# Buffers for split expert weights, and work of the first expert moved ahead, in a sparse attention and MoE kernel on one core

## The chip, the core and the metric

The kernel runs on one core of a Trainium2 chip. Its engines work beside one another, each on its own queue, in order: TensorE (PE) multiplies matrices, VectorE (DVE), ScalarE (ACT) and GpSimd (POOL) work on elements, and the queue of SyncE (SP) issues the DMA transfers. An engine waits for another by a semaphore. The metric is the device time of one execution in microseconds (us); a kernel is judged by the median of its runs.

## What is computed

Block-sparse attention (4 batches, 8 heads, 768 positions, head dimension 64), whose output is the input of a mixture of 8 experts. Every token goes through every expert; the gate's weights are balanced over rows and columns eight times.

```python
scores = scale * np.matmul(q, k.transpose(0, 1, 3, 2))
scores = np.where(mask, scores, -1000000000.0)
scores = scores - np.max(scores, axis=-1, keepdims=True)
attn = np.exp(scores); attn = attn / (np.sum(attn, axis=-1, keepdims=True) + 1e-09)
x = np.matmul(attn, v)                       # then (3072, 512): heads side by side
P = np.exp(x @ w_gate - max)                 # (3072, 8), eight rounds of balancing
...
for e in range(E):
    h = np.maximum(x @ w1[e], 0.0)           # 512 -> 1024
    out += P[:, e:e + 1] * (h @ w2[e])       # 1024 -> 512
```

## The kernel before

**Number form.** A float32 operand is scaled by a power of two and split into two float16 halves, high = f16(s * w) and low = f16(s * w - high). A product is three matmuls (high x high, high x low, low x high). One *split* of a weight quarter is therefore one ACT instruction for the high half and one DVE instruction for the low half.

**Seven products.** Each matrix product of the expert part is done by a seven-product scheme on 2 x 2 quarters, numbered 0 to 6, in the order 0, 1, 5, 6, 3, 4, 2 (`PORDER`). Four quarters of a weight matrix and sums of them give seven operands. The sums are made on POOL, in place over the raw quarters, so some sum must wait until an earlier split has read its quarter: the sums for products 5 and 2 of w1 wait for the splits of 0 and 1, and so do those for 5 and 3 of w2.

**Attention part (0 to 414 us).** A planner issues work tick by tick (`T`), by a table `plan_at` of fixed places and by *chains* of jobs: at the end of every tick, `deal` takes from each chain what is ready and fits an estimate of how busy DVE, ACT and POOL are. Three instructions per tile of the softmax matter here: the exp (`pe`, ACT, line 730), its low part (`pl`, on the engine that the planner thinks lightest, lines 740, 742, 744) and the matmuls with V (line 787). V's raw data lies in `vraw` (line 448). The chains load w1 and w2 of the first expert and find their scales; they sum and split all seven quarters of w1 (`first_sums`, `first_high`, `first_low`, lines 258 to 282), and make the first four of eight sums of w2 (lines 980 to 993).

**Expert part (from 414 us).** An *item* i is one expert and one batch, i = 4e + b, 32 in all. Stage 1 of an item (`stage1`, line 1315) makes the hidden values: 4 column blocks x 7 products x 6 matmuls 128x384, evacuated by DVE (line 1336) and ACT, then split into halves `h` (ACT line 1345; low half DVE line 1350 or 1356, or POOL line 1356). Stage 2 (`stage2`, line 1435) makes the outputs: 7 products x 3 row blocks x 12 matmuls 128x256, which DVE adds into the accumulator (line 1480). The main loop (line 1555) runs stage 2 of item i interleaved with stage 1 of item i + 1. Names such as `p_8_0` mean item 8, column block 0.

**Who sets the order.** `Slots` (line 1109) counts a *tick* for each product and each output block. Work beside the matmuls waits in queues: *urgent* (halves of h), *lazy* (weights: magnitudes, scale, sums, splits, in the order in which they were queued), *calm* (the last batch's x steps, then the gate's balancing). A step runs when its tick has come and the estimate of its engine isn't over TensorE's by more than 1 us. `slots.need(key)` runs at once whatever of a key is left; `stage1` does it for the w1 operand and `stage2` for the w2 operand of a product. A scheduler then orders the instructions of each engine by these places.

**Weights of the next expert.** The raw weight has one buffer (`r`), w1 and w2 in turn. In the second item of an expert (b = 1) w1 of the next is loaded, scaled, and half of its sums made (`sum_w1`). The split operands of w1 have one buffer per product (lines 231 to 242, in the memories `arena` and `attic`). So `split_w1` (line 1216) queues the split of product p only when the last column block of the expert's last stage 1 has used it (`used[p]()`, line 1329); the other sums are queued behind the splits of 0 and 1. w2 is split alike in stage 2 of the last item (`split_w2`, line 1239). For the first expert `split_w2` queues, around its first column blocks, seven splits and the last four sums (two sums of four pieces on POOL, line 1202).

**Last batch's x.** `finish_x` (line 373) makes steps for the fourth batch: differences on POOL (line 401), high halves on ACT (387), low halves on DVE (391) with a store on SP (393), and the gate's logits on TensorE (332). They are queued with delay `LATE` = 34 ticks (line 1529); balancing follows them in the same queue.

## Time and profile before

| | |
|---|---|
| median of 3 runs | 2201.07 us (2196.04 to 2204.06) |
| profiled execution | 2201.64 us |
| its span, first to last instruction | 2199.9 us |
| granted TensorE clock, mean | 0.998 |
| busy: PE, weight loads, DVE, ACT, POOL | 98%, 72%, 78%, 58%, 65% |
| DMA, mean | 87 GB/s |

A row of a group of instructions reads: line, engine, operation, output<-inputs with shapes, count | busy time, mean ns of one | idle time of the engine just before them and what ended most of it. A row of the waits reads: engine and line <- engine and line that it waited for: us in total, times, longest. A row of the timeline has the start, the length, the instruction and count, and in brackets the idle time before it with its releaser. A row of a stretch has its bounds and length, then the busy time and count of PE, weight loads, DVE, ACT and POOL, the granted clock, the DMA share and GB/s. Weight loads run beside matmuls, and the ends of matmuls are modelled.

### The profile page before, as it was taken

To read this page: it belongs to the slowest core of one execution; us is meant where nothing else is said; L and a number is where in the kernel's file an instruction comes from. 1 tells how busy PE (TensorE), PEld (TensorE's weight loads), DVE (VectorE), ACT (ScalarE), POOL (GpSimd) and SP (SyncE) were. 2 spreads that over 40 slices of the span, in tenths; PEclk is the share of its full clock that TensorE was granted. 3 is DMA by queue.
4 is the path that set the end of the run, shared out by engine and by line. 5 is a ranking of instruction groups with operands and counts; after the bars stand their busy time and mean duration, and the time that the engine had idled before them with its cause. 6 is when DMAs were issued, how large, how long until landed. Compare 5 with 4: busy or idle time off the path is not lost.

```text
span 2199.9 us, 47055 instructions
## 1 busy us (share of the span) xinstructions
PE 2150.8 (98%) x18796; PEld 1591.8 (72%) x18796; DVE 1706.8 (78%) x2970; ACT 1282.8 (58%) x2385; POOL 1432.6 (65%) x1476
## 2 busy tenths in 40 slices
PE   6999999999999999999999999999999999999999
PEld 4777676667777777777777777777777777777777
DVE  8889889677878767876887688768876887688765
ACT  5888888666466546554655465546554655465442
POOL 4667768477568656765676567656765686567553
PEclk9999999999999999999999999999999999999999
DMA  6757796122121212121212121212121212131221
GB/s 170 180 130 171 171 198 146 42 100 84 58 89 51 90 51 90 51 90 51 89 52 89 51 89 51 89 51 89 51 89 51 90 51 89 51 90 58 80 80 51
DMA packets 195632, 192.34 MB, mean 87 GB/s; under 512 B 132412, under 2 KB 150868, under 8 KB 195412
## 3 DMA queue, kind: packets, MB, share of 16 engines
q1 hardware_dynamic: 194848, 189.30, 30.6%
q8 instruction: 147, 2.41, 0.4%
q14 instruction: 73, 0.60, 0.1%
q10 hardware_dynamic: 564, 0.03, 0.0%
HBM read 140.54 MB, written 17.30 MB: 72 GB/s over the span
## 4 chain that ended last, share of the span: by engine, by line
PE 72%; DVE 11%; POOL 7%; ACT 4%; issue 4%; DMA 1%; POOLq 0%; DVEq 0%; ACTq 0%
PE py L1456 31%; PE p L1324 30%; PE u L787 3%; PE m L689 2%; PE t L722 2%; PE m L692 2%; PE t L725 2%; POOL h L1356 2%; DVE top L698 1%; ACT h L1345 1%; POOL s L1404 1%; DMA kt<-ks 1%; POOL r L1202 1%; DVE h L1356 1%; DVE attic L1191 1%
## 5 line engine op out<-in xcount | busy, mean ns | idle before, releaser
L1456 PE MATMUL py<-w2p,h 128*128 128x256 f16 x8064 | 973.2, 273 | 6.3 <-DVE acc L1480 2.6
L1456 PEld LDWEIGHTS <-h 128*128 128x128 f16 x8064 | 788.9, 98 | 159.0 <-issue 7.4
L1356 POOL TENSOR_TENSOR h<-u,h 128x384 f16<-128x384 f32 x128 | 126.4, 988 | 534.8 <-ACT h L1345 534.8
L1324 PE MATMUL p<-attic 128*128 128x384 f16 x2304 | 421.4, 326 | 3.9 <-DVE attic L1191 2.1
L1324 PEld LDWEIGHTS <-attic 128*128 128x128 f16 x3072 | 299.2, 98 | 173.1 <-DVE attic L1191 6.6
L1324 PE MATMUL p<-arena 128*128 128x384 f16 x2304 | 417.1, 326 | 4.2 <-DVE arena L1191 1.7
L1480 DVE SCALAR_TENSOR_TENSOR acc<-py,spare,acc 128x256 f32<-128x256 f32 (+1 forms) x588 | 299.8, 514 | 90.9 <-PE py L1456 85.5
L1345 ACT ACTIVATE h<-c 128x384 f16<-128x384 f32 x256 | 132.5, 518 | 348.3 <-DVE c L1336 301.2
L1324 PEld LDWEIGHTS <-arena 128*128 128x128 f16 x2304 | 224.9, 98 | 128.4 <-issue 3.5
L1336 DVE SCALAR_TENSOR_TENSOR a<-p,a 128x384 f32<-128x384 f32 x384 | 211.4, 550 | 20.8 <-PE p L1324 9.0
L1356 DVE TENSOR_TENSOR h<-s,h 128x384 f16<-128x384 f32 x128 | 113.2, 884 | 146.6 <-ACT h L1345 146.5
L698 DVE TENSOR_REDUCE top<-m 128x1 f32<-128x768 f32 x192 | 181.8, 951 | 41.0 <-PE m L692 40.3
L730 ACT ACTIVATE pe<-t,qk 128x768 int32<-128x768 f32 x192 | 172.3, 899 | 69.8 <-PE t L725 58.7
L1209 POOL TENSOR_TENSOR c<-c,r 128x384 f32<-128x384 f32 x128 | 159.1, 1243 | 10.0
L1345 ACT ACTIVATE h<-r 128x384 f16<-128x384 f32 x256 | 129.8, 516 | 60.4 <-POOL r L1209 58.8
L1209 POOL TENSOR_TENSOR r<-s,r 128x384 f32<-128x384 f32 x128 | 157.9, 1234 | 10.0
L744 POOL TENSOR_SCALAR pl<-pe 128x768 f16<-128x768 uint16 x125 | 108.9, 874 | 72.2 <-ACT pe L730 69.7
L1404 POOL TENSOR_TENSOR s<-a,u 128x384 f32<-128x384 f32 x128 | 133.0, 1039 | 30.9 <-ACT a L1401 30.1
L1356 POOL TENSOR_TENSOR h<-r,h 128x384 f16<-128x384 f32 x128 | 146.0, 1140 | 6.0 <-ACT h L1345 6.0
L1324 PE MATMUL p<-arena,attic 128*128 128x384 f16 x768 | 145.9, 326 | 0.0
L787 PE MATMUL u<-vq,pl 128*128 128x65 f16 x1152 | 142.2, 193 | 0.3 <-ACT pl L742 0.3
L689 PE MATMUL m<-kt,qt 128*128 128x512 f16 (+1 forms) x384 | 127.7, 333 | 15.2 <-DMA kt<-ks 10.9
(196 smaller groups left out, 3704.1 us busy)
## 6 DMA issues: line engine op xcount, KB each, us to landing
arena<-xd SPq DMA_DIRECT2D x128, 384.0 KB, 3.4
attic<-xd SPq DMA_DIRECT2D x96, 384.0 KB, 3.6
r<-in_moe_w_dram SPq DMA_DIRECT2D x14, 2048.0 KB, 8.6
arena<-in_q_dram SPq DMA_DIRECT2D x16, 384.0 KB, 4.2
arena<-in_k_dram SPq DMA_DIRECT2D x16, 384.0 KB, 4.6
vraw<-in_v_dram SPq DMA_DIRECT2D x16, 384.0 KB, 5.6
xd<-xs_t SPq DMA_DIRECT2D x16, 384.0 KB, 4.3
out_dram<-acc SPq DMA_DIRECT2D x48, 128.0 KB, 1.7
```

The source lines that it names most:

```text
L689: nc.tensor.matmul(sc[:, lo:hi], lhsT=qt[:, 0, c], rhs=ka[:, lo:hi], start=True, stop=False)
L698: nc.vector.tensor_reduce(out=tops[n][:, c : c + 1], in_=sc[:, :S], axis=AX.X, op=ALU.max)
L730: nc.scalar.activation(pe, sc[:, :S], AF.Exp, bias=EXP_SHIFT, scale=qk[n // 2][3])
L787: nc.tensor.matmul(uv[:, c, :n], lhsT=l[:, c * P : (c + 1) * P], rhs=w[:, h, kc, :n], start=(kc == 0 and c == 0 and m == 0), stop=(kc == N ...
L1209: nc.gpsimd.tensor_tensor(out=out, in0=x, in1=y, op=ALU.subtract)
L1324: nc.tensor.matmul(ps, lhsT=w1p[p][:, l, kc, fs], rhs=xp[p][:, r, kc], start=(kc == 0 and m == 0), stop=(kc == KH - 1 and m == 2),)
L1336: nc.vector.scalar_tensor_tensor(out=t, in0=ps, scalar=HDOWN, in1=other, op0=ALU.mult, op1=ALU.add)
L1345: nc.scalar.activation(h[:, 0], src, AF.Relu if relu else AF.Copy)
L1356: eng.tensor_tensor(out=h[:, 1], in0=src, in1=h[:, 0], op=ALU.subtract)
L1404: nc.gpsimd.tensor_tensor(out=s1, in0=a1, in1=u3, op=ALU.add)
L1456: nc.tensor.matmul(py, lhsT=hs[i, p, kc][:, l, tsl], rhs=w2p[p][:, r, kc], start=(old is None and kc == 0 and m == 0), stop=(kc == KF // 2 ...
L1480: nc.vector.scalar_tensor_tensor(out=dst, in0=src, scalar=c, in1=dst, op0=ALU.mult, op1=ALU.add)
```

## The change

Three edits. (1) Three more buffers for split w1 operands (`spares`). The operands of products 0, 1 and 6 of the next expert go into them as soon as its sums and scale are made, in its second item, with the sums for 5 and 2 in the same queue; only the splits of 5, 3, 4 and 2 follow the last products, into the buffers that products 0, 1, 5 and 6 of the old expert let go. The buffers of its 3, 4 and 2 become the next spares. (2) V's raw memory becomes a tile that lives to the end (`vault`); when the attention is done with V it holds the split w2 operands of products 1, 0 and 5. For the first expert these are split by the planner's chains, after the remaining four sums, which become jobs as well. The planning loop runs 11 ticks longer, `ROOM`. (3) `LATE` goes from 34 to 22.

```diff
-LATE = 34
+LATE = 22
+ROOM = 12
...
+    vault = ctx.enter_context(tc.tile_pool(name="vault", bufs=1)).tile(
+        [P, H * NC * D], F32, name="vault"
+    )
...
+    w2p = {
+        p: carve(4 * KB * n, F16, 2, KF // 2, DH, home=vault)
+        for n, p in enumerate((1, 0, 5))
+    }
...
-        vraw = vsp.tile([P, H, NC, D], F32, name="vraw")
+        vraw = vault.rearrange("p (h c d) -> p h c d", h=H, c=NC)
...
+            by_w2.update({0: m[0, 0], 1: m[1, 0], 5: m[0, 0]})
+            return [
+                add for out, x, y in (
+                    (t1, m[0, 1], m[0, 0]), (m[0, 1], m[0, 1], m[1, 1]),
+                    (m[0, 0], m[1, 1], t1), (m[1, 0], m[1, 0], m[0, 0]),
+                ) for add in add_kc(two(out), two(x), two(y))
+            ]
...
+        for p in (1, 0, 5):
+            until = ((("w2", "power"), 1),) + (
+                ((("w2", "sum", 5), 2),) if p == 5 else ()
+            )
+            splits += [
+                job(("w2", "high", p), lambda p=p: first_high(w2p[p], by_w2[p], 2),
+                    (0.0, 1.14, 0.0), after=until),
...
-        for T in range(min(plan_at), max(plan_at) + 1):
+        for T in range(min(plan_at), max(plan_at) + ROOM):
...
+    w1ps = {0: w1p}
+    spares = [big.tile([P, 2, KH, FH], F16, name=f"w1p_{n}") for n in range(3)]
+    follows = {}
...
     def split_w1(e):
         a, s3 = wr["a"], wr["s3"]
+        old = w1ps[e - 1]
+        new = w1ps[e] = {p: spares.pop(0) for p in (0, 1, 6)}
...
+        one(0, a[0, 0])
+        queue_sum(a[0, 0], a[1, 0], a[0, 0], ("w1", e, 5))
+        one(1, a[0, 1])
+        queue_sum(a[0, 1], a[0, 1], a[0, 0], ("w1", e, 2))
+        one(6, s3)
+        spares.extend(old[p] for p in (3, 4, 2))
...
+        return dict((
+            follow(5, a[0, 0], 0), follow(3, a[1, 1], 1),
+            follow(4, a[1, 0], 5), follow(2, a[0, 1], 6),
+        ))
...
             sum_w1(e + 1)
+            follows[e + 1] = split_w1(e + 1)
```

What stands where, in three places. The line numbers of the changed kernel are a little higher: its lines 286 and 291 are the first expert's high and low halves (276 and 279 before), 742 the exp (730), 1230 the low half of a weight (1191), 1384 the evacuation of a product (1336), 1404 a low half of h (1356), 1528 the addition into the accumulator (1480).

ACT at the end of the attention part, before (`pe_3_7702` to `pe_5_7756` belong to the second last head, the next exps to the last; `xf` is the copy of the transposed output):

```order
L730 ACTIVATE pe_3_7702<-t_3_7697,qk_15_6550 128x768
L730 ACTIVATE pe_4_7729<-t_4_7724,qk_15_6550 128x768
L730 ACTIVATE pe_5_7756<-t_5_7751,qk_15_6550 128x768
L825 ACTIVATE xf_6862<-u_149 128x384
L730 ACTIVATE pe_0_7787<-t_0_7782,qk_15_6550 128x768
L730 ACTIVATE pe_1_7814<-t_1_7809,qk_15_6550 128x768
L730 ACTIVATE pe_2_7841<-t_2_7836,qk_15_6550 128x768
L730 ACTIVATE pe_3_7873<-t_3_7868,qk_15_6550 128x768
L825 ACTIVATE xf_6862<-u_148 128x384
L730 ACTIVATE pe_4_7904<-t_4_7899,qk_15_6550 128x768
L730 ACTIVATE pe_5_7931<-t_5_7926,qk_15_6550 128x768
```

and now (`vault` holds the split w2 operands):

```order
L286 ACTIVATE vault<-r_0_5733,sw_0_5736 128x1024
L742 ACTIVATE pe_4_7733<-t_4_7728,qk_15_6553 128x768
L286 ACTIVATE vault<-r_0_5733,sw_0_5736 128x1024
L742 ACTIVATE pe_5_7763<-t_5_7758,qk_15_6553 128x768
L837 ACTIVATE xf_6865<-u_152 128x384
L742 ACTIVATE pe_0_7796<-t_0_7791,qk_15_6553 128x768
L742 ACTIVATE pe_1_7824<-t_1_7819,qk_15_6553 128x768
L742 ACTIVATE pe_2_7853<-t_2_7848,qk_15_6553 128x768
L742 ACTIVATE pe_3_7886<-t_3_7881,qk_15_6553 128x768
L286 ACTIVATE vault<-r_0_5733,sw_0_5736 128x1024
L837 ACTIVATE xf_6865<-u_151 128x384
L742 ACTIVATE pe_4_7918<-t_4_7913,qk_15_6553 128x768
```

Three high halves have come in between the exps, the third of them ahead of the last two exps.

POOL where the first item's stage 1 ends (`c_0_3`) and the second's begins (`u_1_0`), before:

```order
L1209 TENSOR_TENSOR c_0_3_8376<-c_0_3_8376,r_0_3_8340 128x384
L1356 TENSOR_TENSOR h_8075<-r_0_3_8340,h_8075 128x384
L1356 TENSOR_TENSOR h_8076<-c_0_3_8376,h_8076 128x384
L1202 TENSOR_TENSOR r_0_5730<-r_0_5730,t_0_6342 128x256 x3
L1202 TENSOR_TENSOR r_0_5730<-r_0_5730 128x256 x4
L1356 TENSOR_TENSOR h_8050<-u_1_0_8520,h_8050 128x384
L1404 TENSOR_TENSOR s_1_0_8596<-a_1_0_8471,u_1_0_8520 128x384
```

and now:

```order
L1248 TENSOR_TENSOR c_0_3_8391<-c_0_3_8391,r_0_3_8355 128x384
L1404 TENSOR_TENSOR h_8088<-r_0_3_8355,h_8088 128x384
L1404 TENSOR_TENSOR h_8089<-c_0_3_8391,h_8089 128x384
L1404 TENSOR_TENSOR h_8063<-u_1_0_8535,h_8063 128x384
L1452 TENSOR_TENSOR s_1_0_8605<-a_1_0_8487,u_1_0_8535 128x384
```

The sums over raw w2 (`r_0`), seven pieces here and one earlier, are gone from this queue; they stand in the attention part, as four instructions of twice the width.

DVE at the step from the second to the third expert (item 7 to item 8), before (`attic` and `arena` with `sw_2` are the low halves of split w1 operands):

```order
L1191 SCALAR_TENSOR_TENSOR attic<-r_2_11894,sw_2_11898,attic 128x1024
L1480 SCALAR_TENSOR_TENSOR acc_9853<-py_1_1_13220,spare_11202,acc_9853 128x256
L1480 SCALAR_TENSOR_TENSOR acc_9853<-py_0_0_13280,spare_11202,acc_9853 128x256
L1480 SCALAR_TENSOR_TENSOR acc_9853<-py_1_2_13239,spare_11202,acc_9853 128x256
L1336 SCALAR_TENSOR_TENSOR r_8_0_13269<-p_8_0_13270,a_8_0_13260 128x384
L1336 SCALAR_TENSOR_TENSOR a_8_0_13260<-p_8_0_13295,a_8_0_13260 128x384
L1336 SCALAR_TENSOR_TENSOR u_8_0_13305<-p_8_0_13306,a_8_0_13260 128x384
L1191 SCALAR_TENSOR_TENSOR attic<-r_2_11894,sw_2_11898,attic 128x1024
L1480 SCALAR_TENSOR_TENSOR acc_9853<-py_0_1_13314,spare_11202,acc_9853 128x256
L1356 TENSOR_TENSOR h_8057<-r_8_0_13269,h_8057 128x384
L1336 SCALAR_TENSOR_TENSOR c_8_0_13329<-p_8_0_13330,u_8_0_13305 128x384
L1191 SCALAR_TENSOR_TENSOR attic<-r_2_11894,sw_2_11898,attic 128x1024
```

and now (`w1p_8096` is one of the three new buffers):

```order
L1230 SCALAR_TENSOR_TENSOR w1p_8096<-r_2_11896,sw_2_11900,w1p_8096 128x1024
L1404 TENSOR_TENSOR h_8080<-s_7_3_13181,h_8080 128x384
L1528 SCALAR_TENSOR_TENSOR acc_9865<-py_1_0_13210,spare_11204,acc_9865 128x256
L1404 TENSOR_TENSOR h_8086<-a_7_3_13044,h_8086 128x384
L1528 SCALAR_TENSOR_TENSOR acc_9865<-py_1_1_13227,spare_11204,acc_9865 128x256
L1528 SCALAR_TENSOR_TENSOR acc_9865<-py_1_2_13246,spare_11204,acc_9865 128x256
L1528 SCALAR_TENSOR_TENSOR acc_9865<-py_0_0_13286,spare_11204,acc_9865 128x256
L1384 SCALAR_TENSOR_TENSOR r_8_0_13274<-p_8_0_13275,a_8_0_13265 128x384
L1384 SCALAR_TENSOR_TENSOR a_8_0_13265<-p_8_0_13300,a_8_0_13265 128x384
L1384 SCALAR_TENSOR_TENSOR u_8_0_13308<-p_8_0_13309,a_8_0_13265 128x384
L1404 TENSOR_TENSOR h_8070<-r_8_0_13274,h_8070 128x384
L1528 SCALAR_TENSOR_TENSOR acc_9865<-py_0_1_13317,spare_11204,acc_9865 128x256
```

Before, three of the seven low halves stood in these rows, two of them between the evacuations of the new expert's first products (`p_8_0`); now the last low half stands ahead of them all, and three of the seven stand in item 6.

More of the change, by code (lines that the diff above doesn't have):

```diff
@@ L950, in sum_chain @@
                 job((nm, "sum", k), lambda k=k: run_sum(k), (0.0, 0.0, 1.45), after=marks(k))
-                for k in range(8 if which == 1 else 4)
+                for k in range(8)
             ))
@@ L1074, in tile_sparse_attention_moe @@
     ps_y = mpool("ps_y", 4, space=PSUM)
-    w2p = [big.tile([P, 2, KF // 2, DH], F16, name=f"w2p_{p}") for p in range(NP)]
+    for p in (6, 4, 3, 2):
+        w2p[p] = big.tile([P, 2, KF // 2, DH], F16, name=f"w2p_{p}")
     hfree = [
@@ L1217, in split_w1, with follow, split @@
         a, s3 = wr["a"], wr["s3"]
+        old = w1ps[e - 1]
+        new = w1ps[e] = {p: spares.pop(0) for p in (0, 1, 6)}
         def one(p, src):
-            queue_split(w1p[p], src, ("w1", e, p))
-        def first():
-            one(0, a[0, 0])
-            queue_sum(a[0, 0], a[1, 0], a[0, 0], ("w1", e, 5))
-        def second():
-            one(1, a[0, 1])
-            queue_sum(a[0, 1], a[0, 1], a[0, 0], ("w1", e, 2))
-        def third():
-            one(6, s3)
-            one(5, a[0, 0])
-        return {
-            0: first, 1: second, 6: third,
-            3: lambda: one(3, a[1, 1]), 4: lambda: one(4, a[1, 0]), 2: lambda: one(2, a[0, 1]),
-        }
+            queue_split(new[p], src, ("w1", e, p))
+        one(0, a[0, 0])
[4 more added lines that the diff above has]
+        spares.extend(old[p] for p in (3, 4, 2))
+        def follow(p, src, was):
+            def split():
+                new[p] = old[was]
+                one(p, src)
+            return was, split
+        return dict((
+            follow(5, a[0, 0], 0), follow(3, a[1, 1], 1),
+            follow(4, a[1, 0], 5), follow(2, a[0, 1], 6),
+        ))
     def split_w2(e, r):
@@ L1250, in sums @@
         def sums():
-            one(1, m[1, 0])
             if e:
+                one(1, m[1, 0])
                 queue_sum(t1, m[0, 1], m[0, 0], ("scale", 2, e))
@@ L1256, in first, with second @@
         def first():
-            one(0, m[0, 0])
-            queue_sum(m[0, 0], m[1, 1], t1, ("w2", e, 5))
-            queue_sum(m[1, 0], m[1, 0], m[0, 0], ("w2", e, 3))
+            if e:
+                one(0, m[0, 0])
+                queue_sum(m[0, 0], m[1, 1], t1, ("w2", e, 5))
+                queue_sum(m[1, 0], m[1, 0], m[0, 0], ("w2", e, 3))
+        def second():
+            one(6, m[0, 1])
+            if e:
+                one(5, m[0, 0])
         return [
@@ L1263, in split_w2 @@
             first,
-            lambda: (one(6, m[0, 1]), one(5, m[0, 0])),
+            second,
             lambda: (one(4, t1), one(3, m[1, 0]), one(2, m[1, 1])),
```

36 lines of the change are left out of this document (23 added, 13 removed).

## The prediction

> **What bounds the kernel now.** I read the page first, then busy time by stretch.
>
> ```profile
> PE 2150.8 (98%) x18796; PEld 1591.8 (72%) x18796; DVE 1706.8 (78%) x2970; ACT 1282.8 (58%) x2385; POOL 1432.6 (65%) x1476
> ```
>
> ```profile
> 0.00:414.00 414.00, 384.86 (x5250) 273.81 (x5251) 349.85 (x611) 321.39 (x449) 273.52 (x396) 0.99 0.67 160
> 414.00:500.00 86.00, 80.67 (x609) 55.76 (x606) 67.52 (x105) 54.34 (x108) 62.78 (x57) 1.00 0.25 83
> 500.00:600.00 100.00, 98.76 (x784) 74.36 (x782) 77.70 (x169) 56.14 (x124) 65.21 (x61) 1.00 0.19 62
> 600.00:720.00 120.00, 115.00 (x873) 84.72 (x871) 97.65 (x167) 72.31 (x143) 85.75 (x78) 1.00 0.24 74
> 720.00:2160.00 1440.00, 1435.06 (x10971) 1071.82 (x10970) 1094.82 (x1886) 772.69 (x1551) 935.93 (x877) 1.00 0.23 70
> 2160.00:2199.90 39.90, 36.50 (x323) 31.31 (x320) 19.23 (x36) 5.95 (x12) 9.38 (x10) 0.99 0.17 55
> ```
>
> The columns are length, then busy time of PE, weight loads, DVE, ACT and POOL. The expert part (MoE) starts at 414 us. TensorE is the bound, and the change leaves its matmuls as they are, so only its waits can go. From 414 to 2160 it is idle for 5.33 + 1.24 + 5.00 + 4.94 = 16.5 us: two thirds of that before 720, in the first expert and the step to the second, the rest spread over 26 items of four products and outputs each. The 29.1 us before 414 and the 3.4 us at the end are not touched. That is the ceiling, and it is under 1% of the span.
>
> The idle column understates a wait, because a matmul's end is modelled later than the next one can start. So I price waits from start to start, against the pace of runs without a wait in the chain that ended last:
>
> ```profile
> 666.65 1.95 PE p L1324 x12
> 675.45 5.24 PE py L1456 x48
> ```
>
> A stage 1 matmul (p) paces 1.95 / 12 = 0.1625 us, a stage 2 matmul (py) 5.24 / 48 = 0.109 us. TensorE's timeline around the waits, with the idle time and who ended it in brackets, in the first expert's stage 1:
>
> ```profile
> 447.78 0.27 PE L1456 MATMUL py<-w2p,h 128*128 128x256 f16 x1
> 448.96 1.30 PE L1324 MATMUL p<-arena 128*128 128x384 f16 x7 [0.91 <-DVE u L1336]
> ```
>
> the first expert's outputs:
>
> ```profile
> 459.70 1.79 PE L1324 MATMUL p<-arena 128*128 128x384 f16 x10
> 463.57 0.49 PE L1456 MATMUL py<-w2p,h 128*128 128x256 f16 x3 [2.08 <-ACT w2p L1187]
> ...
> 474.83 0.33 PE L1324 MATMUL p<-attic 128*128 128x384 f16 x1
> 475.91 1.36 PE L1456 MATMUL py<-w2p,h 128*128 128x256 f16 x11 [0.75 <-ACT acc L1477]
> ```
>
> and the steps to the second expert (two waits) and to a later one:
>
> ```profile
> 616.77 2.46 PE L1456 MATMUL py<-w2p,h 128*128 128x256 f16 x21
> 619.95 2.79 PE L1456 MATMUL py<-w2p,h 128*128 128x256 f16 x24 [0.72 <-DVE h L1350]
> ...
> 627.13 0.93 PE L1456 MATMUL py<-w2p,h 128*128 128x256 f16 x7
> 629.81 0.82 PE L1324 MATMUL p<-arena 128*128 128x384 f16 x4 [1.75 <-DVE arena L1191]
> ...
> 1077.56 0.49 PE L1324 MATMUL p<-attic 128*128 128x384 f16 x2
> 1078.48 1.15 PE L1324 MATMUL p<-attic 128*128 128x384 f16 x6 [0.42 <-DVE attic L1191]
> 1079.46 0.93 PE L1456 MATMUL py<-w2p,h 128*128 128x256 f16 x7
> 1080.53 0.82 PE L1324 MATMUL p<-attic 128*128 128x384 f16 x4
> ```
>
> **The change, part by part.**
>
> *Three w2 weights and four sums of the first expert, made in the attention part.* They leave the stretch from 414 to 500. What they do there, from the waits:
>
> ```profile
> ACT w2p L1187 <- POOL r L1202: 2.4, 1, 2.4
> ```
>
> At 461 us TensorE wants the weight of output product 5. ACT has not split it, since POOL still makes the sum that it is split from. Start to start: 3.87 - 10 x 0.1625 = 2.25 us. After the change that weight is ready before stage 1 begins, so this wait goes whole. At 474.8 us ACT copies an output bank late, behind a split: 1.08 - 0.16 = 0.92 us; that split belongs to those moved out or done earlier, and I take all of it. At 447.8 us TensorE waits 1.18 - 0.109 = 1.07 us for a DVE that runs late on h halves; the part keeps two splits there, so I take half, 0.5 (bounds 0 and 1.07). Sum 3.7.
>
> They enter the attention's last 14 us. What stands there, what one of each costs (mean ns after the bar), and the spread of the later experts' sums (shortest, median, longest ns):
>
> ```profile
> 400.00:414.00 14.00, 13.68 (x257) 10.87 (x254) 7.25 (x23) 10.99 (x14) 1.26 (x3) 1.00 0.07 16
> L1187 ACT ACTIVATE w2p<-r,sw 128x1024 f16<-128x1024 f32 x48 | 53.1, 1136 | 7.6 <-DVE sw L225 5.1 <-POOL r L1202 2.4
> L934 POOL TENSOR_TENSOR r<-r 128x512 f32<-128x512 f32 x2 | 3.1, 1578 | 0.0
> L279 DVE SCALAR_TENSOR_TENSOR attic<-r,sw,attic 128x512 f16<-128x512 f32 x6 | 6.3, 1042 | 0.0
> L744 POOL TENSOR_SCALAR pl<-pe 128x768 f16<-128x768 uint16 x125 | 108.9, 874 | 72.2 <-ACT pe L730 69.7 <-DMA xd<-xs_b 0.9
> L1202 POOL TENSOR_TENSOR r<-r x102: 718/1194/2262, 462.3 to 2017.7; 128x256 f32<-128x256 f32 x60, 128x512 f32<-128x512 f32 x42
> ```
>
> POOL gets the four sums and, on balance, two low parts of exp, 4 x 1.58 + 2 x 0.87 = 8.1 us, and has 12.7 free. DVE gets 6 x 1.04 = 6.3 us, loses those two low parts, and has 6.75 free. ACT gets 3 x 1.14 = 3.4 us and has 3.0 free: over by 0.4. Queued behind ACT's third high half, which waits for the POOL sums, are the last two exps; behind the POOL sums is the low part of the second last tile. TensorE waits for both, but three products of stage 1 and one matmul now stand ahead of that tile, 19 x 0.1625 = 3.1 us of cover. So I charge 0.7 us, bounds 0 (all covered) and 3 (if each sum stretches from 1.58 to 2.26, the longest later one, 4 x 0.68 = 2.7 us more, and ACT stands still for them).
>
> *Three more w1 buffers.* Before, expert e+1's seven splits and four of its sums could begin only as the last item's last products let go of the buffers. Now three splits and the sums are made two items sooner, into buffers that nobody reads, and only four follow the products. In the order the two DVE splits that stood between the next expert's first evacuations are gone. The waits they ended:
>
> ```profile
> PE p L1324 <- DVE attic L1191: 2.1, 5, 0.4
> ```
>
> Five of the seven steps between experts look like the one at 1078 us: 0.92 - 2 x 0.1625 = 0.60 there, and 1.07 - 7 x 0.109 = 0.31 two rows on, 0.9 together; five times that is 4.5 us. The first step is worse: at 627 us 2.68 - 7 x 0.109 = 1.92 us for a split into arena, and at 616.8 us 3.18 - 21 x 0.109 = 0.89 us for an h half that DVE reached late behind the same splits. Sum 7.3. What is late next is the ordinary DVE evacuation, which keeps up elsewhere.
>
> The three splits and four sums now run beside ordinary work. The loop that takes them (one item, 55 us) and the loop that loses them, for the second and third expert:
>
> ```profile
> 723.00:778.00 55.00, 55.00 (x424) 41.23 (x423) 37.63 (x74) 33.51 (x74) 36.72 (x35) 1.00 0.17 51
> 834.00:889.00 55.00, 54.45 (x419) 40.58 (x418) 45.91 (x81) 38.38 (x77) 35.92 (x32) 1.00 0.28 86
> L1191 DVE SCALAR_TENSOR_TENSOR arena<-r,sw,arena x21: 1269/1554/2365, 613.6 to 1950.9; 128x1024 f16<-128x1024 f32 x21
> L1202 POOL TENSOR_TENSOR r<-r 128x512 f32<-128x512 f32 x42 | 66.5, 1609 | 0.0
> ```
>
> The taker gets 3 x 1.55 = 4.7 us on DVE, 4 x 1.61 = 6.4 on POOL and 3 x 1.14 = 3.4 on ACT, and has 17, 18 and 21 free; TensorE is never idle there. Cost 0 if all of it is hidden; 0.3 per expert if one wait like the smaller of the two above comes back. I take 0.1, seven times: 0.7.
>
> The same split takes 1.27 us at best and 2.37 at worst. The Trainium skill, page "SBUF — State Buffer", section "Who interferes with whom", says that a DVE instruction with two SBUF inputs and a GpSimd instruction that reads SBUF exclude one another, the later one standing still for the whole of the other. That speaks against putting splits and sums side by side; by it each split could lose a whole sum, and the cost here would be three sums of 1.61 us of DVE time per expert, still within the spare time, so the sum of terms would stay. The trace agrees in kind: the worst split is 1.10 us over the best.
>
> *The x steps 12 ticks sooner.* The same instructions on ACT, DVE, POOL and SP's queue, and the gate's balance behind them, 12 to 16 us earlier (a tick is one product, 6 x 0.1625 = 0.98 us, or one output bank, 12 x 0.109 = 1.31). In the order they do stand earlier. TensorE meets them now in:
>
> ```profile
> PE lg L332 <- DVE xs_b L391: 1.1, 1, 1.1
> ACT xs_t L387 <- POOL xf L401: 5.0, 3, 2.7
> ```
>
> The logits wait 1.1 us for a split, and ACT stands behind a late POOL difference for up to 2.7 us. Both dependences stay, at another place; on SP's queue a third x store now stands ahead of the next loads of x, which are not wanted until the item after. I take 0, bounds a gain of 2.2 (both waits hidden) and a loss of 2.7 (one more of the longer kind). V's new memory and the longer planning loop add no instruction.
>
> **Sum.** 3.7 + 7.3 - 0.7 - 0.7 = 9.6 us. The profiled run took 2201.64 us, 1.74 over its span; the median of the three runs is 2201.07, 0.57 lower, and the waits are the same program's, so I take 9.6 from the median: **2191.5 us**. A measurement of this kernel can tell about 0.5%, 11.0 us: faster means under 2190.1, slower over 2212.1.
>
> **The rivals.**
>
> *Given back (27%).* The steps between experts gain, 4.5 us, but the first 300 us of the MoE part stay crowded: the same x steps, gate and splits press on DVE, and the waits taken off at 461 to 630 us come back at other instructions. For it: DVE is at 97.65 of 120 us from 600 to 720 and the late h halves there have several causes. Against: eight sums and three splits really leave the first 86 us. Price: 2201.07 - 4.5 + 1 to 2 for the tail, about 2198.
>
> *More than counted (20%).* DVE and POOL, relieved in the loops where TensorE now waits, also end waits that I left in: the other half at 447.8 us, both waits of the x steps (2.2), and the 2.8 of the 4.9 us idle after 720 which the five steps' 2.1 do not explain. 2191.5 - 0.6 - 2.2 - 2.8 = 2185.9.
>
> *Splits and sums lock each other (5%), slower.* In the loop that now holds three splits and four sums, every split takes its worst 2.37 instead of 1.27 and every sum stretches as much: 7 x 1.1 = 7.7 us per expert. If TensorE waits for all of it, seven experts cost 54 us: 2191.5 + 54 = about 2245. It decides from 9.6 / 7 = 1.4 us per expert on. Against: beside the same POOL work they cost 0.9 us per step today, in a busier loop. The page named above gives the mechanism, and no row shows the wait reaching TensorE where DVE has room.
>
> **How the numbers follow.** Forecast 48%, its own range 2187 to 2196. The range 2183 to 2200 takes in the second rival below it and the first above it, with the tail's bound; outside are the third rival and stray ends. Faster by over 0.5%: 20% from the second rival, and about a third of the forecast's range (2187 to 2190.1 of 9 us) of 48%, 16%: 0.36. Slower: 0.05. Within: 0.59.
>
> **What would show it.** Right: from 414 to 500 TensorE's idle time falls from 5.3 to about 2 us and no output matmul waits for a w2 split; the 1.92 us wait at the first step and the five pairs of 0.9 are gone; the distance between two steps falls by about 0.9 us; the last 14 us of attention grow by under 1. Wrong: TensorE waiting for a low part or an exp before 420 us by over 2 us; new waits on DVE in the loops that took the splits; or the stretch from 500 to 720 idle as before.

## The result and the profile after

| | before | changed |
|---|---|---|
| median, first comparison (6 runs each) | 2197.98 us | 2185.4 us |
| range of the runs | 2194.85 to 2204.06 | 2183.02 to 2188.84 |
| median, repeated with the last experiments | 2197.83 us | 2182.62 us |
| profiled execution | 2201.64 us | 2183.02 us |
| its span | 2199.9 us | 2181.2 us |

The ratio is 0.9942 with a 95% interval of 0.993 to 0.9954, and 0.9938 (0.9925 to 0.995) in the repetition: by the ratios 12.7 and 13.6 us less, by the medians 12.6 and 15.2. The result lies inside the range of 2183 to 2200, but below the forecast's own 2187 to 2196, and comes nearest to the second rival, "more than counted" (2185.9). Of the 6.1 us between the forecast of 2191.5 and 2185.4, 3.1 come from the kernel before, whose median fell from 2201.07 in three runs to 2197.98 in six.

Busy time by stretch in the profile of the changed kernel; columns as before (length, then PE, weight loads, DVE, ACT, POOL, granted clock, DMA share, GB/s):

```profile
400.00:414.00 14.00, 12.95 (x203) 9.63 (x201) 11.05 (x16) 10.80 (x14) 9.56 (x7) 1.00 0.01 2
414.00:500.00 86.00, 85.58 (x685) 60.70 (x683) 67.22 (x114) 54.26 (x111) 59.13 (x54) 1.00 0.32 105
500.00:600.00 100.00, 96.67 (x744) 72.10 (x742) 82.70 (x177) 57.52 (x124) 68.78 (x61) 1.00 0.13 43
600.00:720.00 120.00, 119.95 (x918) 89.49 (x917) 93.49 (x161) 73.39 (x147) 83.89 (x79) 1.00 0.30 96
720.00:2160.00 1440.00, 1439.75 (x11049) 1080.27 (x11047) 1090.06 (x1894) 772.72 (x1551) 948.66 (x879) 1.00 0.22 69
```

TensorE's idle time falls from 5.33 to 0.42 us in the first expert, from 5.00 to 0.05 at the step to the second, and from 4.94 to 0.25 in all that follows. It rises in two places: in the last 14 us of the attention part (0.32 before, 1.05 now) and from 500 to 600 us (1.24 before, 3.33 now). All of TensorE's waits from 414 us to the end, in the changed kernel:

```profile
PE all_lg L119 <- DVE spare L1323: 1.6, 1, 1.6
PE cs L1341 <- DVE spare L1335: 1.5, 1, 1.5
PE py L1504 <- ACT h L1393: 0.2, 1, 0.2
PE py L1504 <- DVE acc L1528: 0.2, 1, 0.2
PE py L1504 <- DVE h L1398: 0.2, 1, 0.2
```

Five rows and 3.7 us are left. No row names a split (line 1230 or `vault`), so no wait in this view is for weights any more. The two long ones are new in this length (before, the longest wait at the balancing was 0.35 us), and both belong to the gate's balancing: TensorE stands, in its order, at a small matmul whose operand DVE makes late.

**The two profiles differ by more than the change.** The time ahead of the expert part varies by more than the order of the instructions explains (in the two profiles of the changed kernel by 2.3 us, over all of them by 10), so I compare from a point that the change does not touch: the score matmul `t` that the expectations call the 720th, ahead of the tail. Its row, the first matmul of column block 1 (the second of four) of item 0, and the first matmuls of items 2 to 5, in TensorE's timeline before:

```profile
396.93 0.38 PE L722 MATMUL t<-qt,kt 128*128 128x512 f16 x1
...
421.47 0.33 PE L1324 MATMUL p<-arena 128*128 128x384 f16 x1
...
509.16 0.33 PE L1324 MATMUL p<-arena 128*128 128x384 f16 x1
...
566.40 0.32 PE L1324 MATMUL p<-arena 128*128 128x384 f16 x1
...
622.58 0.33 PE L1324 MATMUL p<-arena 128*128 128x384 f16 x1
...
680.52 0.33 PE L1324 MATMUL p<-arena 128*128 128x384 f16 x1
```

and after:

```profile
393.32 0.38 PE L734 MATMUL t<-qt,kt 128*128 128x512 f16 x1
...
420.01 0.49 PE L1372 MATMUL p<-arena 128*128 128x384 f16 x2
...
501.96 0.33 PE L1372 MATMUL p<-arena 128*128 128x384 f16 x1
...
559.43 0.49 PE L1372 MATMUL p<-arena 128*128 128x384 f16 x2
...
616.84 0.33 PE L1372 MATMUL p<-arena,w1p 128*128 128x384 f16 x1
...
671.71 0.33 PE L1372 MATMUL p<-arena,w1p 128*128 128x384 f16 x1
```

The differences between these rows, and the same for the experiments below ("tail" runs from the score matmul to column block 1 of item 0, "to item 2" from there to item 2, and an item from its first matmul to that of the next; the last x step is the last `xs_t` high half of the fourth batch on ACT, counted from the score matmul):

| kernel | tail of attention | to item 2 | item 2 | item 3 | item 4 | item 5 to end | sum | last x step |
|---|---|---|---|---|---|---|---|---|
| before | 24.54 | 87.69 | 57.24 | 56.18 | 57.94 | 1519.4 | 1802.9 | 150.9 |
| changed | 26.69 | 81.95 | 57.47 | 57.41 | 54.87 | 1509.5 | 1787.9 | 125.0 |
| e1, w1 buffers | 24.54 | 87.68 | 57.19 | 61.21 | 56.05 | 1511.9 | 1798.6 | 169.2 |
| e2, w2 part | 26.69 | 81.93 | 56.59 | 56.17 | 57.62 | 1518.9 | 1797.9 | 146.6 |
| e3, x steps | 24.54 | 86.69 | 57.85 | 56.18 | 57.65 | 1519.3 | 1802.2 | 150.5 |
| e4, all but x steps | 26.69 | 81.96 | 56.62 | 61.18 | 56.07 | 1509.9 | 1792.4 | 165.1 |
| e5, gate later | 26.68 | 81.96 | 62.36 | 56.19 | 55.01 | 1509.3 | 1791.5 | 125.7 |
| e6, e4 + later splits | 26.68 | 81.94 | 56.60 | 56.27 | 55.28 | 1509.3 | 1786.1 | 146.7 |
| e7, e1 + x steps | 24.54 | 86.73 | 57.88 | 60.23 | 56.06 | 1511.6 | 1797.0 | 169.0 |
| e8, two w2 products | 25.24 | 85.57 | 57.86 | 61.21 | 56.06 | 1510.0 | 1796.0 | 168.5 |
| e9, later splits | 26.67 | 81.94 | 59.68 | 58.53 | 54.86 | 1511.7 | 1793.4 | 125.7 |
| e10, e1 + later splits | 24.54 | 87.69 | 57.22 | 56.25 | 55.28 | 1511.7 | 1792.7 | 150.9 |
| e11, e8 + later splits, 34 | 25.24 | 85.20 | 57.23 | 56.27 | 55.29 | 1511.0 | 1790.2 | 149.1 |
| e12, changed again | 26.67 | 81.94 | 58.12 | 57.41 | 54.87 | 1509.9 | 1788.9 | 125.7 |

Of the 18.7 us between the two spans, 3.6 stand ahead of the score matmul and are no effect of the change; 15.1 stand behind it, 14.0 in the second profile of the changed kernel (e12). The same program thus differs by 1 us between two profiles, 0.65 of it in item 2.

### The profile page after: what moved, and what is told of

It reads as the page before. It is cut to its first block, busy times and chain, and to the rows that moved or that the text cites. A ratio compares the mean times of both kernels' runs of the same rounds, so it can differ in the third digit from the quotient of the medians.

```text
span 2181.2 us, 47028 instructions
## 1 busy us (share of the span) xinstructions
PE 2146.5 (98%) x18796; PEld 1592.9 (73%) x18796; DVE 1696.5 (78%) x2971; ACT 1282.5 (59%) x2385; POOL 1443.5 (66%) x1474
## 4 chain that ended last, share of the span: by engine, by line
PE 86%; DVE 5%; POOL 4%; ACT 2%; issue 2%; DMA 1%; POOLq 0%; ACTq 0%; DVEq 0%
PE py L1504 37%; PE p L1372 36%; PE u L799 3%; PE t L734 2%; PE m L701 2%; PE t L737 2%; PE m L704 2%; DVE top L710 1%; DMA kt<-ks 1%; POOL h L1404 1%; DVE h L1404 1%; POOL s L1452 0%; ACT h L1393 0%; DVE pl L752 0%; ACT pe L742 0%
## 5 line engine op out<-in xcount | busy, mean ns | idle before, releaser
L1504 PE MATMUL py<-w2p,h 128*128 128x256 f16 x4608 | 564.6, 273 | 0.3 <-DVE acc L1528 0.2
L1404 POOL TENSOR_TENSOR h<-u,h 128x384 f16<-128x384 f32 x128 | 132.5, 1035 | 521.0 <-ACT h L1393 521.0
L1504 PE MATMUL py<-vault,h 128*128 128x256 f16 x3456 | 413.1, 273 | 0.5 <-ACT h L1393 0.2
L1372 PEld LDWEIGHTS <-attic 128*128 128x128 f16 x2208 | 215.8, 98 | 120.6 <-issue 0.9
L1372 PEld LDWEIGHTS <-arena 128*128 128x128 f16 x1728 | 168.8, 98 | 91.3 <-issue 0.6
L1372 PE MATMUL p<-attic 128*128 128x384 f16 x1152 | 212.1, 326 | 0.0
L1372 PE MATMUL p<-arena 128*128 128x384 f16 x1152 | 210.9, 326 | 0.1
L1372 PEld LDWEIGHTS <-w1p 128*128 128x128 f16 x1440 | 140.7, 98 | 77.7 <-issue 0.6
L1372 PE MATMUL p<-arena,attic 128*128 128x384 f16 x1056 | 195.0, 326 | 0.0
L1248 POOL TENSOR_TENSOR r<-s,r 128x384 f32<-128x384 f32 x128 | 157.4, 1230 | 10.0
L1372 PE MATMUL p<-arena,w1p 128*128 128x384 f16 x864 | 161.3, 326 | 0.0
```

What stands on the lines that cost most here:

```text
L1248: nc.gpsimd.tensor_tensor(out=out, in0=x, in1=y, op=ALU.subtract)
L1372: nc.tensor.matmul(ps, lhsT=w1ps[i // B][p][:, l, kc, fs], rhs=xp[p][:, r, kc], start=(kc == 0 and m == 0), stop=(kc == KH - 1 and m == 2),)
L1404: eng.tensor_tensor(out=h[:, 1], in0=src, in1=h[:, 0], op=ALU.subtract)
L1504: nc.tensor.matmul(py, lhsT=hs[i, p, kc][:, l, tsl], rhs=w2p[p][:, r, kc], start=(old is None and kc == 0 and m == 0), stop=(kc == KF // 2 ...
```

## The experiments

All are compared with the kernel before on the same chip, in five rounds each (5 to 12 runs of a kernel). The stretches are from one profile of each.

### The three parts alone, and all but one

e1 has edit (1) alone, e2 edit (2) alone, e3 edit (3) alone; e4 is the changed kernel with edit (3) undone:

```diff
-LATE = 22
+LATE = 34
```

> Only the three w1 buffers; w2's splits and sums and the x steps as before. Theory (the edits take off separate waits and add up): TensorE's idle time from 720 to 2160 us falls from 4.9 to under 1 us, the five pairs of 0.9 us at the steps are gone, the 2.2 us wait at 461 us stays; from 600 to 720 us 2.8 us of idle go. About 7 us faster than before, ratio 0.997. Rival (the first step is relieved by the earlier x steps, not by the buffers): 600 to 720 stays near 5 us idle and the gain is about 4.5 us, 0.998.

> Only the three w2 operands in V's memory and four sums in the attention part. Theory: from 414 to 500 us idle falls from 5.3 to about 0.5 us; the attention's last 15 us grow by 2 (as in the changed kernel's profile, where they grew by 2.2 against an anchor at 397 us); the steps between experts stay as before. About 3 us faster, ratio 0.9985. Rival (the growth at the end of the attention part is only the shorter wait for a transpose ahead of it being given back): no growth there, about 5 us faster, 0.9975.

> Only the x steps 12 ticks sooner. Theory: idle from 500 to 600 us rises from 1.2 to about 3 us, as two matmuls of the gate come to wait for a DVE that is late (1.6 and 1.5 us in the changed kernel), and nothing else moves: 1 to 2 us slower or within 1 us, ratio 1.000 to 1.001. Rival (the x steps are what empties the first step): 600 to 720 us falls by 3 us or more and the kernel is 2 to 4 us faster, 0.9985.

> The changed kernel with the x steps at 34 ticks again. Theory: the two waits of the gate at 523 and 562 us go or shrink, idle from 600 to 720 us stays under 1 us: as fast as the changed kernel or 1 to 2 us faster, ratio to before 0.9935 to 0.994. Rival (the x steps matter for the first step): waits come back from 600 to 720 us, 3 us or more, ratio 0.9955.

| run | median | ratio (95%) |
|---|---|---|
| e1, w1 buffers | 2195.55 us | 0.998 (0.9969 to 0.9992) |
| e2, w2 part | 2194.79 us | 0.9976 (0.9966 to 0.9986) |
| e3, x steps | 2198.27 us | 0.9993 (0.9982 to 1.0003) |
| e4, both without x steps | 2189.09 us | 0.9957 (0.9944 to 0.997) |

Of what was expected, e1, e2 and e4 came out at the rivals' ratios, but not by the rivals' ways: in e1 the idle time from 600 to 720 us did fall, from 5.0 to 2.0 us; in e2 the tail did grow, by 2.15 us; in e4 the waits came back in item 3, ahead of 600 us. e3 has neither the two long waits of the gate nor the 3 us at the first step.

The ratios alone look like parts that add: 4.4 + 5.3 + 1.5 = 11.2 us. The table by stretch shows that they don't. The w1 buffers win 7.5 us from item 5 on and 1.9 in item 4, and lose 5.0 in item 3, which lasts 61.21 us instead of 56.18; e4 loses the same, the changed kernel does not. In item 3 of e1, on TensorE and then on ACT:

```profile
569.88 2.11 PE L1330 MATMUL p<-arena 128*128 128x384 f16 x12
571.83 1.47 PE L1462 MATMUL py<-w2p,h 128*128 128x256 f16 x12
575.81 2.19 PE L1462 MATMUL py<-w2p,h 128*128 128x256 f16 x10 [2.50 <-ACT acc L1483]
```

```profile
569.71 0.84 ACT L387 ACTIVATE xs_t<-xf 128x768 f16<-128x768 f32 x1 [1.37 <-POOL xf L401]
...
572.43 0.52 ACT L1351 ACTIVATE h<-a 128x384 f16<-128x384 f32 x1 [1.24 <-POOL a L1212]
573.69 0.52 ACT L1351 ACTIVATE h<-r 128x384 f16<-128x384 f32 x1 [0.74 <-POOL r L1212]
574.50 0.45 ACT L1284 ACTIVATE pw<-lg,spare 128x192 f32<-128x192 f32 x1 [0.28 <-DVE spare L1283]
...
575.39 0.91 ACT L1483 ACTIVATE acc<-py 128x256 f32<-128x256 f32 x3
```

TensorE waits 2.50 us for a bank that ACT copies out. ACT has it last in a row of instructions that wait, in order, for POOL and DVE, and that begins with the last x step, itself 1.37 us late behind POOL, and has the gate's exp (`pw`) in it. In the kernel before this step ran 19 us ahead of item 3:

```profile
547.82 0.84 ACT L387 ACTIVATE xs_t<-xf 128x768 f16<-128x768 f32 x1 [2.66 <-POOL xf L401]
```

And the wait costs more than itself. Two stretches of four microseconds in e1; the third column from the right is the granted clock:

```profile
572.00:576.00 4.00, 1.50 (x14) 1.20 (x13) 3.20 (x7) 2.54 (x7) 3.84 (x5) 0.99 0.53 173
576.00:580.00 4.00, 4.00 (x21) 2.56 (x20) 3.05 (x9) 1.73 (x5) 0.66 (x1) 0.58 0.07 26
```

Right behind the wait TensorE is granted 0.58 for four microseconds: 0.42 x 4 = 1.7 us more of running time. Not all of it lengthens the item: e7 below has the same wait without the half clock, and its item 3 is 1.0 us shorter (60.23). So a new theory: in the planner's queues the early splits of the second expert go ahead of the x steps and fill the engines' estimates, the last x step and the gate's start are pushed to the start of item 3, and that costs 5 us.

### The splits one item later

e6 leaves the x steps at 34 ticks and queues only the second expert's early splits one item later:

```diff
-LATE = 22
+LATE = 34
...
-            follows[e + 1] = split_w1(e + 1)
+            if e:
+                follows[e + 1] = split_w1(e + 1)
+        if i == 2:
+            follows[1] = split_w1(1)
```

> The changed kernel with the x steps at 34 ticks, and for the second expert alone the three early w1 splits and their sums queued one item later (in the third item of the first expert), so that they stand behind the last x step. Theory (the early splits of the second expert push the last x step and the gate's start from 19 us ahead of item 3 to its very start, where TensorE stands 2.5 us behind ACT and is then granted half its clock): the last high half of x on ACT comes at about 545 us again, item 3 lasts 56 to 57.5 us instead of 61.2, no slice of it is granted under 1.00, ratio to the kernel before about 0.994. Rival (the splits' own load on DVE and ACT makes the wait, wherever they stand): item 3 or item 4 lasts 60 us or more, ratio 0.9957 as with 34 ticks before.

2183.39 us, ratio 0.9934 (0.9919 to 0.9949), against 0.9957 for e4. ACT's row for the last x step, and TensorE's first of items 3 and 4:

```profile
538.73 0.84 ACT L399 ACTIVATE xs_t<-xf 128x768 f16<-128x768 f32 x1 [2.65 <-POOL xf L413]
```

```profile
557.29 0.32 PE L1372 MATMUL p<-arena 128*128 128x384 f16 x1
...
613.56 0.33 PE L1372 MATMUL p<-arena,w1p 128*128 128x384 f16 x1
```

The step runs 18.6 us ahead of item 3 again and the item lasts 56.27 us. The rival (the splits' own load makes the wait, wherever they stand) is out: the same load one item later costs nothing there.

Why the step lands just there can be read from the kernel. In e1, e4, e7 and e8 it starts 0.17 us ahead of item 3's first matmul, with 34 ticks and with 22. There the main loop, at `i == 2`, calls `finish_late`, whose `slots.need(("late", 0, 0))` runs at once what is left of the x steps. The splits are in the lazy queue, which `Slots` serves ahead of the calm one; the last step finds no room until this deadline, and the gate's work behind it starts as late.

e10 does the same to the w1 buffers alone:

> The kernel before with the three w1 buffers alone (x steps at 34 ticks, w2 as before), the second expert's early splits queued one item later. Theory (the buffers alone gave 4.4 us only because their splits push the last x step and the gate to the start of item 3): item 3 lasts 56 to 57.5 us instead of 61.2, and from the second column block to the end it gains about 9 us over the kernel before, ratio 0.996. Rival (the buffers are worth 4.4 us whatever the x steps do): ratio 0.998 as with the buffers alone.

2189.2 us, ratio 0.9963 (0.9951 to 0.9976), item 3 56.25 us. Behind the score matmul the buffers alone now win 10.2 us, instead of 4.4; by the ratios 8.1.

### The x steps sooner, with the buffers and without

e7 is e1 with `LATE = 22`; e9 is the changed kernel with the splits of e6.

> The kernel before with the three w1 buffers and the x steps at 22 ticks, without the w2 part. Theory (the two edits belong together): from the second column block of the first item to the end it gains 9 us over the kernel before (4.4 for the buffers alone, 4.5 for the 12 ticks once the buffers are there), ratio 0.9958. Rival (the parts add): 4.4 + 0.8 = 5.2 us, ratio 0.9977.

> The changed kernel (x steps at 22 ticks) with the second expert's three early w1 splits queued one item later. Theory (all that matters is that the last x step stands ahead of the early splits): it stands ahead of them with either delay, at about 518 us here, so no wait over 2 us at the start of item 3; of the changed kernel's two gate waits the first (1.77 us, ahead of any early split) stays and the second (1.67 us, behind them) shrinks; ratio to the kernel before 0.9934 to 0.9942, as with 34 ticks and later splits. Rival (the 12 ticks have a worth of their own): 2 us or more better than with 34 ticks, 0.9925 or less.

e7: 2195.26 us, ratio 0.9984 (0.9973 to 0.9995). My theory expected 0.9958 and is wrong in this point, and the rival (the parts add, 0.9977) is within the interval: without the w2 part the shorter delay does not bring the last x step forward. It stands 169.0 us behind the score matmul, as in e1 (169.2), and item 3 lasts 60.23. e3 says the same from the other side: 150.5 with the shorter delay, 150.9 without. There the first high half does come 19 us sooner behind the score matmul (73.8 instead of 92.5), but its low half on DVE then stands until 92.6. The delay isn't what holds the last steps. By the code it is the estimate in `Slots` (a step runs only when it fits), and that has room only when the w2 work has left too; the estimate itself was not read out. Then 12 ticks move the last step by 40 us: 165.1 in e4, 125.0 in the changed kernel.

e9: 2186.72 us, ratio 0.996 (0.9947 to 0.9973), above the 0.9934 to 0.9942 that I expected; the rival (a gain by the 12 ticks of their own) is out. The second gate wait did not shrink, it grew to 2.25 us now that the splits stand beside the balancing, and item 3 lasts 58.53 us:

```profile
581.49 0.39 PE L1341 MATMUL cs<-spare,ones 128*128 128x8 f32 x2 [2.25 <-DVE spare L1335]
```

Of the 59.68 us of item 2 that is no sign: its two waits (0.49 and 1.61 us) are in e12 too (0.51 and 1.60), where the item lasts 58.12, and behind them this profile has 3.4 us at half the clock (shown at the end). Another 2 us stand from item 5 on, at waits of another kind that come and go (below).

### The tail of the attention part

e8 makes only the products 1 and 0 of w2 in the attention part. The third, and the last two of the four sums, go back to the expert part:

```diff
-                    (m[0, 0], m[1, 1], t1), (m[1, 0], m[1, 0], m[0, 0]),
...
-        for p in (1, 0, 5):
+        for p in (1, 0):
```

> The changed kernel with only two w2 products (1 and 0) split in the attention part; the third split and the last two sums of w2 stay in the expert part, as before the change. Theory (the tail of attention is lengthened by POOL's sums and DVE's low halves of exp, which stretch from 0.56 to 1.3 us beside each other): the three low halves at the end take 0.56 us again, the stretch from the 720th score matmul to the second column block of the first item goes from 26.69 to 25.3 us (24.54 before), the 0.68 us of the POOL low half beside the first splits staying. Rival (ACT, over by 0.4 us with three high halves, makes the tail): it falls by a third at most, to 26.0. The first expert may lose up to 2.25 us at product 5 again; ratio to the kernel before 0.9935 if it does not, 0.9945 if it does.

> Two w2 products in the attention part, x steps at 34 ticks, the second expert's early splits one item later. Theory (the loss of the two-product kernel in the expert part was the last x step, pushed to the start of item 3 again): item 3 lasts 56 to 57.5 us, the attention's tail stays at 25.2 us, the 1.3 us wait for the third product at 460 us stays; together the time of three products with later splits, ratio 0.9934. Rival (the third product itself is worth it): the wait at the start of item 3 stays, ratio 0.9975.

e8: 2192.07 us, ratio 0.9981 (0.9969 to 0.9994). The tail fell to 25.24 us, as the theory had it. In the changed kernel, TensorE, DVE and POOL:

```profile
404.89 0.20 PE L799 MATMUL u<-vq,pl 128*128 128x65 f16 x1 [0.52 <-POOL pl L756]
...
408.08 0.20 PE L799 MATMUL u<-vq,pl 128*128 128x65 f16 x1 [0.19 <-DVE pl L752]
...
411.17 0.20 PE L799 MATMUL u<-vq,pl 128*128 128x65 f16 x1 [0.17 <-DVE pl L752]
```

```profile
407.20 3.92 DVE L752 TENSOR_SCALAR pl<-pe 128x768 f16<-128x768 uint16 x3
```

```profile
403.51 1.33 POOL L756 TENSOR_SCALAR pl<-pe 128x768 f16<-128x768 uint16 x1 [0.56 <-ACT pe L742]
404.80 2.80 POOL L946 TENSOR_TENSOR r<-r,t 128x512 f32<-128x512 f32 x2
407.56 3.14 POOL L946 TENSOR_TENSOR r<-r 128x512 f32<-128x512 f32 x2
```

and in e8, DVE at the same place:

```profile
410.34 0.55 DVE L752 TENSOR_SCALAR pl<-pe 128x768 f16<-128x768 uint16 x1
...
413.06 0.56 DVE L752 TENSOR_SCALAR pl<-pe 128x768 f16<-128x768 uint16 x1 [1.12 <-ACT pe L742]
```

Three low halves of exp take 3.92 / 3 = 1.31 us beside POOL's sums and 0.56 without them, and TensorE then waits for each of them. Taken one by one in the trace, each ends 0.42 us after a sum ends. From start to start the three waits are 1.1 of the 26.69 - 25.24 = 1.45 us between the two kernels. The other 0.33 is order and no loss: three transposes of `xn`, ahead of column block 1 in the changed kernel and behind it in e8 and before. Of the tail's 2.15 us, 0.70 stays in e8, whose POOL low halves still run beside DVE's first splits (1.26 and 1.32 us there, 1.33 above; 0.874 on the mean in the kernel before). The rival (ACT's three high halves) expected 26.0 at best and is out; the exps of these three low halves also start at the same distance from the score matmul in both kernels (11.14, 12.71 and 13.91 us). The Trainium skill, page "SBUF — State Buffer", section "Who interferes with whom", says that an operation such as tensor_scalar can run in a mode that takes the ports which DVE shares with GpSimd, and that the one that comes first then holds them for its whole length. The stretch of 0.56 to 1.31 us beside sums of 1.57 us, and the ends just behind those of the sums, fit that; which mode these instructions ran in no run here shows.

The ratio missed the 0.9945 that I expected at worst. That is the x steps once more: without the third product's work gone, the last one stands at 168.5 and item 3 lasts 61.21 us. e11 undoes that with later splits: 2185.39 us, ratio 0.9953 (0.9939 to 0.9966), item 3 56.27 us. It came 4.1 us behind e6 in the traces, where I expected the same (0.9934): the third product is worth 85.20 - 81.94 = 3.3 us in the first expert, not 1.3, against 1.44 in the tail. Of the rest, 1.7 us stand from item 5 on.

### The gate's waits

e5 tries to take the two new waits away, by an earlier maximum and longer gaps:

```diff
-        slots.add(weigh, ("balance",), 1, True, dve=0.5)
+        slots.add(most, ("balance",), 1, True, dve=0.3)
+        slots.add(weigh, ("balance",), 4, True, dve=0.3, gap=4)
...
-            slots.add(lambda it=it: cols(it), ("balance",), 2, True, dve=0.9, gap=3)
+            slots.add(lambda it=it: cols(it), ("balance",), 2, True, dve=0.9, gap=4)
```

> The changed kernel, with the first step of the gate's balancing (maximum over a row) put apart from the one that spreads the maximum by a small TensorE matmul, four ticks before it, and the column matmuls four ticks instead of three behind the row steps. Theory (TensorE stands in order at a small gate matmul whose operand DVE makes late): the two waits of the changed kernel, 1.77 us at 523.6 and 1.67 us at 561.9 from start to start, go, 3.4 us; ratio to the kernel before 0.9927 (0.9942 less 3.4 of 2198). Rival (DVE has no room there, whatever the order): the waits come back at other instructions of that DVE queue, ratio 0.994 as the changed kernel.

2189.49 us, ratio 0.9962 (0.9948 to 0.9977), above the changed kernel in both of its measurements, and in the table 3.6 us longer. The wait at the first small matmul went, and the next two gate matmuls took its place:

```profile
543.38 0.39 PE L1343 MATMUL cs<-spare,ones 128*128 128x8 f32 x2 [1.19 <-DVE spare L1337]
...
561.09 0.39 PE L1343 MATMUL cs<-spare,ones 128*128 128x8 f32 x2 [1.80 <-DVE spare L1337]
```

The waits came back at other instructions of the same queue, as the rival had it, but the time is above the rival's 0.994 too. About half of the 3.6 us may be chance: behind the 1.80 us wait this profile has 3.4 us at half the clock.

### The changed kernel again

> The changed kernel itself, beside the three others on the same chip. Ratio to the kernel before 0.9942, as first measured. If the theory of the x steps holds, it is within 0.1% of the two kernels with three w2 products and later splits.

2182.62 us, ratio 0.9938 (0.9925 to 0.995). e6 (0.9934) reaches the same time by another way, as expected; e9 (0.996) does not, and that half of the expectation failed. No version beats the changed kernel by what can be measured.

## Why the prediction came out as it did

The terms, as they were put, and what the stretches of the table say (gains positive):

| term | predicted | by the table's stretches | put to its term |
|---|---|---|---|
| w2 work out of the first expert | 3.7 | 5.7 | 5.4 |
| tail of the attention part | -0.7 | -2.15 | -1.8 |
| x steps sooner, and the gate (items 2 and 3) | 0 | -1.5 | -2.4 |
| first step between experts (item 4) | 2.8 | 3.1 | 4.0 |
| later steps, less the early splits' cost | 4.5 - 0.7 | 9.9 | 9.9 |
| sum | 9.6 | 15.1 | 15.1 |

The last column moves two things that stand on the other side of a border: the three transposes (0.33 us), and the 0.89 us wait at 616.8 us, which belongs to the first step but stands in item 3.

The forecast was right in its mechanism, the waits for splits and sums, and 12.6 to 15.2 us were won where it said 9.6. Its terms missed in both directions, and the misses partly cancelled: the gains came out 8.3 us larger than it said and the costs 2.8 us. The larger gains are of the kind that the second rival named, waits that the sum had left in.

- **The first expert.** All three waits at 447.8, 461 and 474.8 us went or shrank, as reckoned. What I left in went too: the second half of the 1.07 us, and the 1.1 us of the logits for a split of x. With them the working gives 2.25 + 0.92 + 1.07 + 1.15 = 5.4, as measured. e2, which has the w2 part alone, gets the whole of it.
- **The tail.** The mechanism that the prediction weighed under the page on SBUF, and priced only where the w1 splits stand, worked here. I took the low halves of exp at their undisturbed time and bounded the stretch of the sums instead. The bound of 3 held; the value of 0.7 was well under half of the truth, and the sign "the last 14 us grow by under 1" failed.
- **The x steps.** This step failed in its form, though the loss stayed inside its bound of 2.7. I took the 12 ticks as a shift of 12 to 16 us that costs and wins nothing, and added the parts. Alone they shift the last step by 0.4 us (e3). With both other parts they move it by 40, away from a collision that the w1 buffers themselves create: the early splits of the second expert, priced at 0.1 us by the engines' spare time, cost about 5 us where they push the x steps to their deadline. I had not seen that, and that the change held the edit that avoids it was luck for the forecast. In the profiles the 12 ticks are worth 4.5 us there (1792.4 - 1787.9 between e4 and the changed kernel), about 1 of it the half clock of e4; by the ratios 3.3 to 4.2, with intervals that overlap. The rival "given back" named the place and the pressure on DVE, and 3.1 us of waits did come back there, at the gate; its time of 2198 is out.
- **The first step.** Both waits that the prediction priced went. The other 1.2 us stood, before, at the only other wait over 0.25 us of item 4, 0.62 us idle at 662 us for the magnitudes of w2 (`ma_w`), which the sum had left out.
- **The later steps.** Item by item behind the first step, in us (one profile of each; all other items from 6 to 30 take 54.81 to 54.87 in these kernels):

| items | before | changed | e1, w1 buffers | e2, w2 part | gain |
|---|---|---|---|---|---|
| 5 | 57.26 | 55.14 | 55.73 | 57.27 | 2.1 |
| 8, 12, 16, 20, 24, 28 | 55.74 to 55.78 | 54.87 | 54.87 | 55.73 to 55.78 | 5.4 in all |
| 9, 13, 17, 21, 25, 29 | 55.46 (9: 55.88, 25: 54.97) | 54.96 to 54.98 (21: 55.50) | 55.46 (21: 54.87) | 54.95 to 55.96 | 2.3 in all |

  The second row is the term that I reckoned: 0.9 us at a step, gone with the w1 buffers and untouched by the w2 part. But all six later steps pay it, not the five whose wait names a split into `attic`. The cost of the early splits, 0.7, was nothing from the third expert on: the items that take them (6, 10, ..., 26) last 54.87 in both kernels. The first row is three waits that have no counterpart after:

```profile
687.76 1.14 PE L1324 MATMUL p<-attic 128*128 128x384 f16 x6 [0.55 <-ACT a L1371]
695.25 1.14 PE L1324 MATMUL p<-arena 128*128 128x384 f16 x6 [0.81 <-DVE a L1336]
704.71 1.47 PE L1456 MATMUL py<-w2p,h 128*128 128x256 f16 x12 [0.49 <-DVE acc L1480]
```

  They stand at ordinary evacuations, about 50 us and more behind the last split of w1 (638.1 us) and among the splits and sums of the second expert's w2. e1 has the same w2 splits without these waits, so the buffers end them; how is open. DVE was not simply behind from the w1 splits, for it is idle for half of the time from 640 to 650 us. The third row is one wait of TensorE for an addition into the accumulator (0.24 us idle), 22.4 us into the item (item 9 of the kernel before has a second one). It comes and goes between two profiles of one program: in item 21 of the changed kernel, in 25 and 29 of e12, in all six of e9. So the 2.3 us are partly chance, and so are 1.8 of the 2.4 us by which the changed kernel is ahead of e1 from item 5 on.
- **Splits and sums lock each other.** The stretch with the early splits, 723 to 778 us, still has TensorE busy for all of its 55 us, and no wait for a split is left. The rival is out for the steps between experts; work of DVE and POOL that stretches side by side cost 1.8 us in the attention's tail, where it is needed at once.

## What to carry to other kernels

Parts of a change that share a planner's queues don't add: look where each of them puts the instructions of the others, by the order of every part alone and of all together, before their gains are summed. The waits that name a split are only a part of what can go with them: of 9.9 us won in the later items, 5.4 stood at the steps and 4.4 at ordinary evacuations and additions. A delay in ticks does not place a step that waits for room; look for the deadline that does. Where DVE and GpSimd work is moved side by side, price the stretch at the instruction that TensorE waits for next, not at the one that was moved.
